# A block-causal attention with a squared-ReLU MLP on one core: the block products get banks of their own, v's scale two VectorE steps, the weight sums a later place, and the order list is planned anew

## The chip, the core and the metric

One core of a Trainium2 chip runs the whole program. The metric is the device time of one execution in microseconds (us). Engines are named as in the profile: PE is TensorE's matmul side and PEld its weight load, DVE is VectorE, ACT is ScalarE, POOL is GpSimd, SP issues the DMAs.

## The reference

Attention over 8 batches, 8 heads, 576 positions and 64 channels, with a mask by blocks of 64, and then an MLP without bias over the 4608 rows that come out:

```python
scores = scale * np.matmul(q, k.transpose(0, 1, 3, 2))
mask = block_i >= block_j
scores = np.where(mask, scores, -1000000000.0)
attn = np.exp(scores - np.max(scores, axis=-1, keepdims=True))
attn = attn / (np.sum(attn, axis=-1, keepdims=True) + 1e-09)
x = np.matmul(attn, v)            # to (4608, 512)
h = x @ w_in                      # (512, 2048)
r = np.maximum(h, 0.0)
out = (r * r) @ w_out             # (2048, 512)
```

q and k are drawn about five times larger than unit-scale noise of 0.1 would be; all is float32.

## The kernel before, in words

Every float32 operand of a large matmul is split in two float16 parts, high and low, and three products (high*high, high*low, low*high) stand for one float32 product. The work falls into 40 **passes** of attention (a pass is a pair of heads of one batch and some of the nine 64-row blocks) and 12 **chunks** of 384 rows of the MLP. Weights come in while the first passes run, are scaled, and are split too.

The order on each engine is a list. `plan_all` adds some 3,000 named steps, each with the engines that may take it, a duration in ns, the steps before it, a rank, and the buffer rings that it takes and frees; `Plan.run` walks through them with those durations and writes one list for each engine, and the compiled program keeps these lists. The constants at the top (`W0`, `YR`, `CHAIN`, `LOADS`, ...) are ranks and costs of this walk. Each engine works its list in order, so a step that waits holds up all that stand behind it.

Names of steps, with the tiles by which the profile shows them:

- In a pass i with groups g: `A` scores on PE into `side`; `B` row maxima on DVE (`nmx`); `C` exponentials on ACT (`p`), which also leave the sums; `S` on POOL (`sm`); `R` reciprocal on DVE (`rs`); from pass 12 on `H` and `L`, the high and low parts (`p_rows`), `T` their transposes by DMA (`p_turned`), and `G` the product with v on PE (`px`). In passes 0 to 11 `D` scales, `E` turns on PE, `F` copies back.
- v's scale, from pass 12 on: `fv` sums of |v| on ACT, `fa` a transpose on PE (`pm`), `fb` on DVE, `fc` a broadcast on PE, `fd` on DVE, then `vh` and `vl`, v's high and low parts (ACT and DVE). Before, `fb` is three DVE instructions (`mx` maximum, `mx` exponent mask, `dg`) and `fd` three more (`m`, `s`, `xsc`).
- Weights: `bits` on POOL, `prelu` on ACT, `join` on DVE rebuild the words; `w0a` to `w0e` and `w1a` to `w1e` make the scale of w_in and of w_out; `cast` and `low` split (DVE 0.5 and 0.7 us each).
- A chunk is **plain** (the first five of the order) or **split** (the other seven). Plain: `ph` (12 matmuls, `pair`), `pos`, `sqr`, `top`, `rem` (ACT and DVE, `r` and `hidden`), then `po` (48 matmuls for each third of the rows, 16 steps of 3), `ob` (scale, DVE) and `out` (store).
- Split chunks replace `ph` by seven block products for eight (a Strassen-Winograd scheme): in each of four groups `p1 p2 p6 p5 p7 p4 p3`, 12 matmuls each, into two banks, X and B. Between them copies take X (`c11`, `c12`, `c22`, `c21`) and additions take B (`a11`, `a22`, `a12`) to `r`: p6 adds to X once c11 has read it, p5 starts B anew once a11 has read it, and so on. The scheme wants sums of weight blocks, `t0_0` to `t3_12` and `t0_13` to `t3_17` (tile `_AluOpType.subtract`, on DVE or POOL).

The banks. PSUM has two tensors `side0` and `side1` of two banks each, `pair0` and `pair1` of one bank, and two banks of pool `ps_x`. From pass 14 on the scores use `side0` alone, and the block products turn through three banks, the halves of `side1` and `pair1`:

```python
homes = {"mm": pairs, "po": pairs[:1], "g": [sides[1][:, 0:512], sides[1][:, 512:1024], pairs[1]]}
```

Semaphores are set by the framework from what instructions read and write of a tensor, and the list's waits are what it finds.

Of the kernel before, what the change touches and what calls it, by code (L numbers as in the profile page):

```python
# [8 lines left out]
F32 = mybir.dt.float32  # L9
F16 = mybir.dt.float16  # L10
BF16 = mybir.dt.bfloat16
I32 = mybir.dt.int32
# [21 lines left out]
CALM = 537.27  # L34
# [19 lines left out]
W0 = (2.5, -14.69, -56.55, 10.59, 73.82, 23.78, 99.37)  # L54
W1 = (853.21, -0.0, -38.79, 11.96, -25.48)
NORMS = (7.15, -223.95)
YR = (62.35, -10.14, 23.9, -41.43)
UR = (281.66, -1.47, 123.95)
SLACK = 0
EARLY = 694.63  # L60
BEGIN = 334.95
FILLER = 10000
CHAIN = 138.99
FRONT = 239.18
MARGIN = 0
LATE = 167.03
LAND = 300
TURN = (699.23, 9.28)
LOADS = "z2 p0 r8 z1 r2 z0 r11 r1 r12 K1 r0 p1 r4 r5 r15 p2 p3 r14 K0 r3 z4 z5 Y0 z6 r13 Y1 r9 r10 r7 z3 r6"
# [64 lines left out]
class Plan:  # L134


    LAG = {"PE": 250, "DVE": 180, "ACT": 220, "POOL": 200, "SP": 100}
# [12 lines left out]
    def run(self):  # L150
# [63 lines left out]
def attention_moe_kernel(ctx: ExitStack, tc: tile.TileContext, qk1, v1, qk, ks, vm, vt, w_in, w_out, out):  # L214
# [12 lines left out]
    turns_of = dict.fromkeys(homes, 0)  # L227
# [255 lines left out]
    def front(t):  # L483
# [6 lines left out]
        def v_sum():  # L490
# [3 lines left out]
            box["steps"] = pow2_steps(box["st"], 1, u)  # L494

        def step(n):
            return lambda: box["steps"][n]()

        def scales():
            m = box["steps"][3]()  # L500
            box["s"] = scale_of(m, A_ATT, 1, u)
            xsc = t["xsc"] = small.tile([P, 1], F32, tag="xsc", name=f"xsc_{u}")
            nc.vector.tensor_scalar(xsc, m, 2.0 ** (-A_ATT - A_P), None, op0=ALU.mult)
# [5 lines left out]
        def v_low():  # L509
# [6 lines left out]
            v_sum=v_sum, turned=step(0), largest=step(1), spread=step(2), scales=scales, v_high=v_high, v_low=v_low  # L516
# [585 lines left out]
    def out_steps(ck, t):  # L1102
# [16 lines left out]
        def scaled(uv):  # L1119
            ob = box["ob"] = p2.tile([P, 512], F32, tag="ob", name=f"ob_{ck}_{t}", bufs=3)  # L1120
            nc.vector.tensor_scalar(
# [32 lines left out]
    def plan_all():  # L1154

        plan = Plan(
            {"s0": 1, "s1": 1, "mm": 2, "x": 2, "p32": 2, "ks": 2, "v16": 2, "g": 3, "po": 1, "qk": 2, "r": 8, "hb": 2, "ob": 3, "dg": 1}
# [56 lines left out]
        def part_steps(wi, f, early, rank):  # L1214
# [23 lines left out]
            add(f"prelu{k}", "ACT", 610, [raw] + back, early, start, takes)  # L1238
# [7 lines left out]
            add(f"low{k}", "DVE", 750, [f"cast{k}"], rank, lambda: box["s"][3](), frees=ends)  # L1246

        def row_steps(t, k, group, rank, after, frees, parts):
# [12 lines left out]
            score = 0.9 * w + 120 if t["quad"] else 880 if short else 1.68 * w + 80 * n - 20  # L1261
# [9 lines left out]
            add(f"R{k}", "DVE", 190, [f"S{k}"], rank, get("inverse"))  # L1271
# [157 lines left out]
        def moe(n):  # L1429
# [7 lines left out]
            for g in range(0 if plain(ck) else NQ):  # L1437
# [27 lines left out]
                for name, after in (("11", f"p1{k}"), ("12", f"p6{k}"), ("22", f"p7{k}")):  # L1465
                    add(f"c{name}{k}", {"ACT": 440, "DVE": 480}, 0, [after], r, step("c" + name), ("r",))
                add(f"a11{k}", "DVE", 560, [f"p2{k}", f"c11{k}"], r, step("a11"))
                add(f"a22{k}", "DVE", 560, [f"p5{k}", f"c22{k}"], r, step("a22"))
                add(f"a12{k}", "DVE", 560, [f"p3{k}", f"c12{k}"], r, step("a12"), frees=[(f"p2{k}", "g")])
                add(f"c21{k}", {"ACT": 440, "DVE": 480}, 0, [f"p4{k}"], r, step("pos"), ("r",), frees=[(f"p1{k}", "g")])  # L1470
                for name in ("11", "21", "22", "12"):
                    first = f"c21{k}" if name == "21" else f"a{name}{k}"
                    add(f"sq{name}{k}", {"ACT": 540 if name == "21" else 1050, "DVE": 520}, 0, [first], CALM, step("s" + name))
# [5 lines left out]
            for f in range(NF if plain(ck) else 0):  # L1479
# [17 lines left out]
                add(f"pos{k}", "ACT", 500, [f"ph{k}"], r, step(1), ("r",), frees=[(f"ph{k}", "mm")])  # L1497
                add(f"sqr{k}", "ACT", 550, [f"pos{k}"], r, step(2))
# [6 lines left out]
            for m in range(3):  # L1505
# [6 lines left out]
                for f in range(NF):  # L1512
# [11 lines left out]
                    f"ob{ck}_{m}", "DVE", 730, [f"po{ck}_{m}_15", f"uv{ck}"], CHAIN, lambda box=box: box["s"][1](uv["a"]),  # L1524
# [12 lines left out]
        for n in range(NQ):  # L1537
# [72 lines left out]
        for t in passes[WHOLE:]:  # L1610
# [27 lines left out]
            add(f"fb{i}", "DVE", 620, [f"fa{i}"], r, go("largest"), ("dg",))  # L1638
            add(f"fc{i}", "PE", 100, [f"fb{i}"], r, go("spread"), frees=[(f"fb{i}", "dg")])
            add(f"fd{i}", "DVE", 470, [f"fc{i}"], r, go("scales"), frees=[(f"fa{i}", "x")])  # L1640
            ready_rows = [f"load{i}"]
            slots = [(f"load{i}", x) for x in ("qk", "ks")]
            add(f"vh{i}", "ACT", 720, [f"fd{i}"], r + (2 if early else 20), go("v_high"))
# [82 lines left out]
```

## Time and profile before

| | us |
|---|---|
| runs, median of 3 | 1044.79 (1043.6 to 1045.23) |
| profiled execution, its own time | 1046.3 |
| its span, first to last instruction | 1044.5 |
| PE busy | 976.9 (94%) |
| DVE busy | 818.7 (78%) |
| ACT busy | 572.4 (55%) |
| POOL busy | 168.7 (16%) |

The profiled execution is 1.5 us above the median of the runs, and 1.8 us of its time lie outside the span. Busy time is the union of an engine's instructions. A matmul row lasts until its modelled end, and the next starts before that, so back-to-back matmuls overlap in the rows.

### The profile page before, as it was taken

The numbers are of one execution on the slowest core, as the hardware profiler recorded it, in microseconds if no ns is written. First come the engines' busy times: TensorE is split into PE (matmuls) and PEld (weight loads), VectorE is DVE, ScalarE is ACT, GpSimd is POOL, SyncE is SP. The second block draws the span as 40 slices with busy tenths as digits, with TensorE's granted clock in tenths as the row PEclk, the third lists the DMA queues.
The fourth block names the chain that finished last, engine by engine and source line by source line (L and its number), as shares of the span: only waits on it lengthen the run. The fifth ranks groups of instructions, "written<-read, shape, count | busy, mean of one in ns | idle before, by whom it ended". The sixth has DMA issues, their size and how long they took to land.

```text
span 1044.5 us, 20623 instructions
## 1 busy us (share of the span) xinstructions
PE 976.9 (94%) x7889; PEld 591.9 (57%) x7889; DVE 818.7 (78%) x1974; ACT 572.4 (55%) x1451; POOL 168.7 (16%) x252
## 2 busy tenths in 40 slices
PE   6679998899999999998999999999999999989998
PEld 5445533444554554554476485586575485486673
DVE  7999899898788777879789687799788787665350
ACT  5888715763874685475455465456566446233130
POOL 3443334220110010003012011011001001011010
PEclk9689999999999999999999999999999999999999
DMA  9852206855665667641624603841963533500001
GB/s 354 311 172 95 96 11 153 184 113 118 143 147 132 148 114 161 131 110 60 144 50 106 135 12 81 177 104 24 211 128 56 112 84 50 98 11 12 21 1 31
DMA packets 216611, 114.86 MB, mean 110 GB/s; under 512 B 190400, under 2 KB 198592, under 8 KB 216512
## 3 DMA queue, kind: packets, MB, share of 16 engines
q1 hardware_dynamic: 216512, 113.54, 44.8%
q8 instruction: 62, 1.02, 0.4%
q14 instruction: 37, 0.30, 0.1%
HBM read 58.20 MB, written 9.44 MB: 65 GB/s over the span
## 4 chain that ended last, share of the span: by engine, by line
PE 61%; DVE 20%; issue 9%; ACT 5%; DMA 2%; POOL 1%; SPq 0%; POOLq 0%; DVEq 0%; ACTq 0%
PE pair L106 37%; PE side L106 18%; PE px L106 5%; DVE w L106 4%; DVE p_rows L106 4%; DVE r L106 3%; DVE nmx L106 3%; ACT r L106 2%; DVE xt_all L106 1%; DMA p_turned<-p_rows 1%; ACT p L106 1%; DVE hidden L106 1%; PE po L106 1%; DVE _AluOpType.subtract L106 1%; DMA w<-in_w_in 1%
## 5 line engine op out<-in xcount | busy, mean ns | idle before, releaser
L106 PE MATMUL pair<-w,hidden 128*128 128x512 f16 x1680 | 384.5, 380 | 2.8 <-DVE ob L106 1.5
L106 PEld LDWEIGHTS <-hidden 128*128 128x128 f16 x1728 | 162.3, 98 | 194.4 <-issue 15.6
L106 PEld LDWEIGHTS <-w 128*128 128x128 f16 x2304 | 203.5, 98 | 97.9 <-issue 38.6
L106 PE MATMUL pair<-xt_all,w 128*128 128x384 f16 (+1 forms) x1392 | 209.5, 304 | 2.6 <-DVE xt_all L106 1.7
L106 ACT ACTIVATE p<-side,nmx 128x256 f32<-128x256 f32 (+8 forms) x264 | 139.6, 539 | 123.2 <-DVE nmx L106 74.4
L106 DVE TENSOR_REDUCE nmx<-side 128x1 f32<-128x64 f32 (+8 forms) x288 | 123.2, 480 | 13.5 <-PE side L106 13.5
L106 DVE SCALAR_TENSOR_TENSOR p_rows<-p,rs,p_rows 128x64 f16<-128x64 f32 (+6 forms) x264 | 133.0, 548 | 0.6
L106 POOL TENSOR_SCALAR sm<-sm 128x2 f32<-128x2 f32 (+2 forms) x104 | 31.2, 300 | 512.7 <-ACT p L106 494.0
L106 ACT CAST hidden<-r 128x384 f16<-128x384 f32 x181 | 91.5, 510 | 35.9 <-DVE r L106 32.2
L106 PE MATMUL side<-qk 64*64 64x512 f32 (+1 forms) x480 | 98.6, 506 | 10.6 <-ACT p L106 9.6
L106 PE MATMUL side<-xt_all,w 128*128 128x192 f16 x912 | 86.2, 246 | 13.3 <-DVE r L106 8.7
L106 PE MATMUL side<-ks,qk 64*64 64x192 f32 (+4 forms) x576 | 93.1, 429 | 0.0
L106 DVE TENSOR_TENSOR hidden<-r,hidden 128x384 f16<-128x384 f32 x144 | 80.0, 562 | 14.1 <-ACT hidden L106 13.0
L106 PEld LDWEIGHTS <-turned_w 128*128 128x128 f16 x1008 | 84.1, 98 | 10.6 <-issue 7.8
L106 POOL TENSOR_TENSOR hidden<-r,hidden 128x384 f16<-128x384 f32 x48 | 48.5, 1015 | 232.8 <-ACT hidden L106 206.8
L106 DVE TENSOR_SCALAR p_rows<-p,rs 128x256 f16<-128x256 f32 (+10 forms) x198 | 76.2, 423 | 2.5
L106 ACT ACTIVATE r<-pair 128x384 f32<-128x384 f32 x106 | 51.6, 489 | 45.2 <-PE pair L106 44.9
L106 PE MATMUL px<-p_turned,v 128*64 128x384 f16 (+5 forms) x1168 | 71.6, 270 | 4.1 <-ACT x L106 1.7
L106 ACT ACTIVATE r<-side 128x384 f32<-128x384 f32 x55 | 26.6, 490 | 85.8 <-PE side L106 80.3
L106 PE MATMUL side<-xt_all,turned_w 128*128 128x192 f16 x684 | 65.1, 246 | 4.6 <-ACT r L106 2.4
L106 DVE TENSOR_SCALAR ob<-pair,uv 128x512 f32<-128x512 f32 x35 | 28.3, 808 | 51.9 <-PE pair L106 51.5
L106 PEld LDWEIGHTS <-v 128*64 128x64 f16 x1128 | 51.4, 110 | 28.3 <-issue 18.8
(149 smaller groups left out, 1126.6 us busy)
## 6 DMA issues: line engine op xcount, KB each, us to landing
qk<-in_qk SPq DMA_DIRECT2D x32, 576.0 KB, 4.5
ks<-in_ks SPq DMA_DIRECT2D x32, 320.0 KB, 4.7
vraw<-in_vm SPq DMA_DIRECT2D x30, 256.0 KB, 5.0
w<-in_w_out SPq DMA_DIRECT2D x10, 512.0 KB, 5.2
out<-ob SPq DMA_DIRECT2D x20, 256.0 KB, 2.0
w<-in_w_in SPq DMA_DIRECT2D x8, 512.0 KB, 8.4
hidden<-in_w_in SPq DMA_DIRECT2D x6, 512.0 KB, 9.9
out<-ob SPq DMA_DIRECT2D x24, 128.0 KB, 2.5
```

The lines of the kernel that those rows point to most:

```text
L106: i = make(*a, **k)
```

## The change

Four things. (1) `side1` and `pair1` move to a pool that is closed at the first block product, and three tensors `group0` to `group2` of one bank each take their place. (2) v's scale: DVE keeps the maximum (`fb`) and one mask step (`fd`), and three small instructions go to POOL as a new step `fe`. (3) The first weight sum waits for the end of pass 16 (`X16_1`). (4) The plan has other durations, new constants and ranks, a penalty of 98.64 ns on DVE where a step may go to several engines (`EASE`), a charge on DVE for paired POOL work (`DRAG`), another order of loads, 500 ns more between a step and a PE step of rank 300 or more (`MARGIN`, `LATE`), and `ob` may go to ACT as two passes.

```diff
-MARGIN = 0
-LATE = 167.03
+DRAG = 0.3
+LATER = 16
+EASE = 98.64
+MARGIN = 500
+LATE = 300
-LOADS = "z2 p0 r8 z1 r2 z0 r11 r1 r12 K1 r0 p1 r4 r5 r15 p2 p3 r14 K0 r3 z4 z5 Y0 z6 r13 Y1 r9 r10 r7 z3 r6"
+LOADS = "p0 p1 p2 r1 p3 r0 Y0 r3 r4 r5 r2 z0 r6 K0 r10 r7 r11 r13 r9 r12 K1 r8 z1 z2 r14 r15 Y1 z3 z6 z4 z5"
...
-                if best is None or at + queues[q] < best[0]:
-                    best = at + queues[q], at, q
+                cost = at + queues[q] + (EASE if q == "DVE" else 0)
+                if best is None or cost < best[0]:
+                    best = cost, at, q
...
+            if q == "POOL" and name.startswith(self.PAIRED) and free["DVE"] > at:
+                free["DVE"] += DRAG * queues[q]
...
-    sides = [ps_b.tile([P, 1024], F32, name=f"side{n}") for n in range(2)]
-    pairs = [ps_b.tile([P, 512], F32, name=f"pair{n}") for n in range(2)]
-    homes = {"mm": pairs, "po": pairs[:1], "g": [sides[1][:, 0:512], sides[1][:, 512:1024], pairs[1]]}
+    early = ExitStack()
+    ps_e = early.enter_context(tc.tile_pool(name="ps_e", bufs=1, space=PSUM))
+    sides.append(ps_e.tile([P, 1024], F32, name="side1"))
+    pairs.append(ps_e.tile([P, 512], F32, name="pair1"))
+    homes = {"mm": pairs, "po": pairs[:1]}
...
+        if ring not in homes:
+            early.close()
+            ps_g = ctx.enter_context(tc.tile_pool(name="ps_g", bufs=1, space=PSUM))
+            homes[ring] = [ps_g.tile([P, 512], F32, name=f"group{n}") for n in range(3)]
...
+        def largest():
+            box["top"] = small.tile([1, 1], BF16, tag="top", name=f"top_{u}", bufs=1)
+            nc.vector.tensor_reduce(box["top"], box["pm"][:1, :P], axis=AX.X, op=ALU.max)
...
+        def read():
+            m = box["m"] = small.tile([P, 1], F32, tag="m", name=f"m_{u}")
+            nc.vector.tensor_scalar(
+                m.bitcast(I32), box["pm"][:, P : P + 1].bitcast(I32), EXPMASK, None, op0=ALU.bitwise_and
+            )
...
+            nc.gpsimd.tensor_scalar(m, m, 2.0**-100, None, op0=ALU.max)
...
+            if q == "ACT":
+                nc.scalar.activation(ob, box["po"], AF.Copy, scale=uv[:, 0, t : t + 1])
+                nc.scalar.activation(ob, ob, AF.Copy, scale=uv[:, 1, t : t + 1])
+                return
...
-                    after += [...] + (["low1_15"] + [f"max1_{f}" for f in range(NF)] if n == 0 else [])
+                    after += [...] + (["low1_15"] + [f"max1_{f}" for f in range(NF)] + [f"X{LATER}_1"] if n == 0 else [])
```

Where the lists move, at three places. First DVE's list around the end of pass 15 and the start of pass 16, before; `p_rows` rows are H and L, `nmx` is B, and the `t_AluOpType.subtract` and `turned_w` rows are weight sums of group 3:

```order
L106 TENSOR_TENSOR t_AluOpType.subtract_2354<-t_AluOpType.subtract_2354,w_99 128x512 x2
L106 RECIPROCAL rs_3_3_4_2384<-sm_3_3_4_2357 128x2
...
L106 SCALAR_TENSOR_TENSOR p_rows<-p_1_3_3_4_2356,rs_3_3_4_2384,p_rows 128x256
L106 TENSOR_TENSOR turned_w<-t_AluOpType.subtract_2354,turned_w 128x2x256
L106 TENSOR_TENSOR t_AluOpType.subtract_2354<-t_AluOpType.subtract_2354,w_99 128x512 x2
L106 TENSOR_REDUCE nmx_0_0_4_2416<-side_73 128x1 x4
L106 TENSOR_SCALAR nmx_0_0_4_2416<-nmx_0_0_4_2416 128x4
L106 TENSOR_TENSOR turned_w<-t_AluOpType.subtract_2354,turned_w 128x2x256
L106 TENSOR_TENSOR t_AluOpType.subtract_2354<-w_99,t_AluOpType.subtract_2354 128x512
L106 TENSOR_TENSOR t_AluOpType.subtract_2354<-t_AluOpType.subtract_2354,w_99 128x512
```

The same place of DVE's list now:

```order
L109 RECIPROCAL rs_3_3_4_2265<-sm_3_3_4_2237 128x2
L109 TENSOR_SCALAR p_rows<-p_1_3_3_4_2236,rs_3_3_4_2265 128x320
L109 TENSOR_SCALAR p_rows<-p_1_3_3_4_2236,rs_3_3_4_2265 128x256
L109 SCALAR_TENSOR_TENSOR p_rows<-p_1_3_3_4_2236,rs_3_3_4_2265,p_rows 128x320
L109 TENSOR_TENSOR hidden<-r_10_2256,hidden 128x384
L109 SCALAR_TENSOR_TENSOR p_rows<-p_1_3_3_4_2236,rs_3_3_4_2265,p_rows 128x256
L109 SCALAR_TENSOR_TENSOR v_2_0_0_2201<-vraw_86,s_0_0_2261,v_2_0_0_2201 128x640
L109 TENSOR_REDUCE nmx_0_0_4_2301<-side_73 128x1 x4
```

The weight sums are gone from here; they stand behind pass 16. Up to the last low part of pass 16 (L16_2_1) the list of before has 20 of them on DVE, that of now none; POOL's list has 20 of the first 52 of these steps before and 27 now.

Second, DVE's list at v's scale in pass 14. Before, six instructions:

```order
L106 TENSOR_REDUCE mx_2_3_1910<-pm_2_3_1891 1x1
L106 TENSOR_SCALAR mx_2_3_1910<-mx_2_3_1910 1x1
L106 TENSOR_SCALAR dg_2_3_1913<-ident,mx_2_3_1910 1x1
...
L106 TENSOR_SCALAR m_2_3_1941<-pm_2_3_1891 128x1
L106 TENSOR_SCALAR s_2_3_1943<-m_2_3_1941 128x1
L106 TENSOR_SCALAR xsc_2_3_1945<-m_2_3_1941 128x1
```

Now two, with other work between them, and m, s and xsc are three rows of POOL's list:

```order
L109 TENSOR_REDUCE top_2_3_1861<-pm_2_3_1702 1x1
L109 TENSOR_REDUCE nmx_2_3_8_1866<-side_73 128x1 x2
L109 TENSOR_SCALAR nmx_2_3_8_1866<-nmx_2_3_8_1866 128x2
L109 TENSOR_TENSOR sq_1_0_1843<-sq_1_0_1843 128x384
L109 TENSOR_SCALAR m_2_3_1882<-pm_2_3_1702 128x1
```

Third, PE's list with its waits in the split chunk 8, where p2 of group 3 (`p28_3`) starts. Before, it stands right behind p3 of group 2, which goes to `pair`:

```order
L106 LDWEIGHTS w_99
L106 MATMUL pair_76<-xt_all,w_99 128x192
L106 LDWEIGHTS w_99
L106 MATMUL side_74<-xt_all,w_99 128x192 [waits Activation_49]
L106 LDWEIGHTS w_99
L106 MATMUL side_74<-xt_all,w_99 128x192
```

Now p2 of group 3 stands behind p1 of group 3, p5 of group 2 and a small `nq` product:

```order
L109 MATMUL group_5469<-xt_all,w_102 128x192
L109 LDWEIGHTS ones_bf
L109 MATMUL nq_1_9386<-sq_1_0_9165,ones_bf 128x384 [waits DVE_49]
L109 LDWEIGHTS ones_bf
L109 MATMUL nq_1_9386<-sq_1_2_9316,ones_bf 128x384 [waits DVE_49]
L109 LDWEIGHTS w_102
L109 MATMUL group_5468<-xt_all,w_102 128x192 [waits Activation_49]
```

Followed to the instruction whose count the semaphore reaches, the wait of before is for the copy c12 of group 3, which reads the other half of `side1`; the wait of now is for c21 of group 2, the last reader of p2's own bank. The products' own work is the same in both lists.

## Rows read from the trace of the kernel before

**Rows 1.** Busy time by stretch (us: PE, PEld, DVE, ACT, POOL; PE's clock, DMA).

```profile
0.00:265.00 265.00, 227.64 (x1567) 124.29 (x1571) 241.69 (x538) 170.69 (x442) 83.73 (x120) 0.94 0.54 161
265.00:488.00 223.00, 220.92 (x1653) 116.60 (x1645) 177.41 (x468) 142.92 (x367) 27.14 (x45) 1.00 0.58 129
488.00:1044.50 556.50, 528.31 (x4676) 351.01 (x4674) 399.63 (x970) 258.79 (x643) 57.85 (x87) 1.00 0.36 78
```

**Rows 2.** The chain that ended last (start, us, what): steps of PE.

```profile
114.48 1.95 PE pair L106 x12
...
262.56 2.19 PE px L106 x42
...
1030.14 10.37 PE pair L106 x48
```

**Rows 3.** PE's waits from 488 to 1044.5 us: in total, times, longest.

```profile
PE side L106 <- DVE r L106: 10.9, 23, 1.1
PE side L106 <- ACT r L106: 7.0, 13, 1.1
...
PE pair L106 <- DVE ob L106: 1.5, 3, 0.6
```

**Rows 4.** Timeline of chunk 8: block products, and copies on ACT (start, us, what).

```profile
779.81 1.15 PE L106 MATMUL side<-xt_all,w 128*128 128x192 f16 x12
780.80 1.15 PE L106 MATMUL pair<-xt_all,w 128*128 128x192 f16 x12
...
784.98 0.49 ACT L106 ACTIVATE r<-side 128x384 f32<-128x384 f32 x1 [2.23 <-PE side L106]
...
786.48 0.48 ACT L106 ACTIVATE r<-side 128x384 f32<-128x384 f32 x1
787.01 1.15 PE L106 MATMUL side<-xt_all,w 128*128 128x192 f16 x12 [1.08 <-ACT r L106]
```

**Rows 5.** DVE's groups by form, 170 to 254 us (count, busy us, mean ns, idle).

```profile
L106 DVE TENSOR_TENSOR _AluOpType.subtract<-_AluOpType.subtract,w 128x512 f32<-128x512 f32 x10 | 6.9, 691 | 0.3
L106 DVE SCALAR_TENSOR_TENSOR p_rows<-p,rs,p_rows 128x384 f16<-128x384 f32 x4 | 4.3, 1064 | 0.0
L106 DVE TENSOR_SCALAR p_rows<-p,rs 128x320 f16<-128x320 f32 x4 | 3.2, 795 | 0.1
L106 DVE TENSOR_SCALAR ob<-pair,uv 128x512 f32<-128x512 f32 x3 | 2.4, 801 | 0.7 <-PE pair L106 0.7
```

**Rows 6.** DVE's groups by form, whole span: small steps of v's scale.

```profile
L106 DVE TENSOR_SCALAR dg<-ident,mx 1x1 bf16<-1x1 f32 x28 | 5.7, 204 | 1.0
L106 DVE TENSOR_SCALAR s<-m 128x1 int32<-128x1 int32 x28 | 4.3, 154 | 1.0
L106 DVE TENSOR_SCALAR xsc<-m 128x1 f32<-128x1 f32 x28 | 4.0, 144 | 0.0
L106 DVE TENSOR_SCALAR mx<-mx 1x1 int32<-1x1 int32 x28 | 4.0, 142 | 1.0
```

**Rows 7.** DVE's timeline: the first scores' maxima, the first reciprocal, the last split of w_out.

```profile
5.70 0.69 DVE L106 TENSOR_REDUCE nmx<-side 128x1 f32<-128x192 f32 x3 [4.09 <-PE side L106]
12.87 0.16 DVE L106 RECIPROCAL rs<-sm 128x3 f32<-128x3 f32 x1
139.76 0.75 DVE L106 SCALAR_TENSOR_TENSOR w<-turned_w,wsc,w 128x512 f16<-128x512 f32 x1
```

**Rows 8.** ACT by form, whole span: one pass over 512 columns.

```profile
L106 ACT ACTIVATE wt<-hidden 128x512 f32<-128x512 f32 x6 | 3.9, 671 | 0.0
```

**Rows 9.** POOL by form, whole span: a small step, and a weight sum.

```profile
L106 POOL TENSOR_SCALAR sm<-sm 128x2 f32<-128x2 f32 x48 | 15.4, 320 | 237.8 <-ACT p L106 231.9 <-DVE hb L106 5.6
L106 POOL TENSOR_TENSOR _AluOpType.subtract<-_AluOpType.subtract,w 128x512 f32<-128x512 f32 x10 | 14.0, 1401 | 2.2 <-DVE _AluOpType.subtract L106 0.8 <-DVE rs L106 0.8
```

**Rows 10.** DVE by form, whole span: H over 320 columns. And the 50 us from 150.

```profile
L106 DVE TENSOR_SCALAR p_rows<-p,rs 128x320 f16<-128x320 f32 x23 | 10.5, 457 | 0.7
...
150.00:200.00 50.00, 43.14 (x269) 20.74 (x269) 45.45 (x95) 27.71 (x63) 21.39 (x20) 0.93 0.59 138
```

More of the change, by code (lines that the diff above doesn't have):

```diff
@@ L33 @@
 ALONE = 14
-CALM = 537.27
+CALM = 17.25
 A_ATT = 14
@@ L493, in v_sum, with turned, spread @@
             nc.scalar.activation(t["v16"][:, 0, :, 0:c, :], v32, AF.Abs, accum_out=box["st"])
-            box["steps"] = pow2_steps(box["st"], 1, u)
-        def step(n):
-            return lambda: box["steps"][n]()
-        def scales():
-            m = box["steps"][3]()
-            box["s"] = scale_of(m, A_ATT, 1, u)
+        def turned():
+            pm = box["pm"] = ps_x.tile([P, 512], F32, tag="x", name=f"pm_{u}")
+            nc.tensor.transpose(pm[:1, :P], box["st"], ident)
+        def largest():
+            box["top"] = small.tile([1, 1], BF16, tag="top", name=f"top_{u}", bufs=1)
+            nc.vector.tensor_reduce(box["top"], box["pm"][:1, :P], axis=AX.X, op=ALU.max)
+        def spread():
+            nc.tensor.matmul(box["pm"][:, P : P + 1], ones_bf[:1], box["top"], start=True, stop=True)
+        def read():
[3 more added lines that the diff above has]
+            )
+        def scales():
+            m = box["m"]
+            nc.gpsimd.tensor_scalar(m, m, 2.0**-100, None, op0=ALU.max)
+            s = box["s"] = small.tile([P, 1], F32, tag="s", name=f"s_{u}")
+            nc.gpsimd.tensor_scalar(
+                s.bitcast(I32), m.bitcast(I32), -1, (254 + A_ATT) << 23, op0=ALU.mult, op1=ALU.add
+            )
             xsc = t["xsc"] = small.tile([P, 1], F32, tag="xsc", name=f"xsc_{u}")
-            nc.vector.tensor_scalar(xsc, m, 2.0 ** (-A_ATT - A_P), None, op0=ALU.mult)
+            nc.gpsimd.tensor_scalar(xsc, m, 2.0 ** (-A_ATT - A_P), None, op0=ALU.mult)
         def v_high():
@@ L515, in front @@
         return dict(
-            v_sum=v_sum, turned=step(0), largest=step(1), spread=step(2), scales=scales, v_high=v_high, v_low=v_low
+            v_sum=v_sum, turned=turned, largest=largest, spread=spread, read=read, scales=scales, v_high=v_high, v_low=v_low
         )
@@ L1237, in part_steps @@
             add(f"bits{k}", "POOL", 800, [raw], early + 10, lambda: low_bits(raws[wi][f]))
-            add(f"prelu{k}", "ACT", 610, [raw] + back, early, start, takes)
+            add(f"prelu{k}", "ACT", 580, [raw] + back, early, start, takes)
             add(
@@ L1245, in part_steps @@
             add(f"cast{k}", {"ACT": 630, "DVE": 520, "POOL": 1600}, 0, [f"join{k}", f"w{wi}e"] + last, rank, lambda q: box["s"][2](q))
-            add(f"low{k}", "DVE", 750, [f"cast{k}"], rank, lambda: box["s"][3](), frees=ends)
+            add(f"low{k}", "DVE", 700, [f"cast{k}"], rank, lambda: box["s"][3](), frees=ends)
         def row_steps(t, k, group, rank, after, frees, parts):
@@ L1465, in moe @@
                 for name, after in (("11", f"p1{k}"), ("12", f"p6{k}"), ("22", f"p7{k}")):
[L1466 to L1470, printed above, removed]
+                    add(f"c{name}{k}", {"ACT": 400, "DVE": 480}, 0, [after], r, step("c" + name), ("r",))
+                add(f"a11{k}", "DVE", 480, [f"p2{k}", f"c11{k}"], r, step("a11"))
+                add(f"a22{k}", "DVE", 480, [f"p5{k}", f"c22{k}"], r, step("a22"))
+                add(f"a12{k}", "DVE", 480, [f"p3{k}", f"c12{k}"], r, step("a12"), frees=[(f"p2{k}", "g")])
+                add(f"c21{k}", {"ACT": 400, "DVE": 480}, 0, [f"p4{k}"], r, step("pos"), ("r",), frees=[(f"p1{k}", "g")])
                 for name in ("11", "21", "22", "12"):
                     first = f"c21{k}" if name == "21" else f"a{name}{k}"
-                    add(f"sq{name}{k}", {"ACT": 540 if name == "21" else 1050, "DVE": 520}, 0, [first], CALM, step("s" + name))
+                    add(f"sq{name}{k}", {"ACT": 440 if name == "21" else 880, "DVE": 520}, 0, [first], CALM, step("s" + name))
                     add(f"top{name}{k}", {"ACT": 440}, 0, [f"sq{name}{k}"] + over[name], r, lambda name=name, step=step: step("h" + name)("ACT"))
@@ L1637, in plan_all @@
             add(f"fa{i}", "PE", 120, [f"fv{i}"], r, go("turned"), ("x",))
[L1638 to L1640 removed]
+            add(f"fb{i}", "DVE", 210, [f"fa{i}"], r, go("largest"), ("top",))
+            add(f"fc{i}", "PE", 100, [f"fb{i}"], r, go("spread"), frees=[(f"fb{i}", "top")])
+            add(f"fd{i}", "DVE", 130, [f"fc{i}"], r, go("read"), frees=[(f"fa{i}", "x")])
+            add(f"fe{i}", "POOL", 800, [f"fd{i}"], r, go("scales"))
             ready_rows = [f"load{i}"]
             slots = [(f"load{i}", x) for x in ("qk", "ks")]
[L1643 removed]
+            add(f"vh{i}", "ACT", 720, [f"fe{i}"], r + (2 if early else 20), go("v_high"))
             add(f"vl{i}", "DVE", 800, [f"vh{i}"], r + (2 if early else 20), go("v_low"))
```

41 lines of the change are left out of this document (22 added, 19 removed).

## The prediction, made before the changed kernel was run

> **What bounds the kernel now.** I read busy time by stretch first [rows 1]; the reader is to see three regimes. Up to 265 us TensorE is busy for 227.6 us and VectorE for 241.7 (91%): this front is VectorE's. From 265 to 488 us TensorE is busy for 220.9 of 223.0 and nothing can be gained but what is in the list itself. From 488 us on, where the split chunks run, TensorE is idle for 556.5 - 528.3 = 28.2 us although VectorE has 157 us to spare. Then the chain that ended last [rows 2], which gives what a step costs when nothing waits: 48 matmuls of `po` in 10.37 us, so 0.648 for a step of three, and 1.95 for a `ph`. Then TensorE's waits in the last stretch [rows 3]: 36 waits of block products for copies of `r` make 17.9 of the 28.2 us. Last the timeline of one of them [rows 4], to see for which copy it waits.
>
> All changes keep TensorE's work, so only its waiting can change. Ahead of any step, its waiting is the step's start less the work that its list has before it. Summing the list, each kind at its unhindered start-to-start time, gives 199.6 us ahead of the product of pass 16; that starts at 262.56 [rows 2], so 63 us have been lost by then. The whole list is 929 us. The other losses are 7 us up to 488 and 41 after it (the part by which these exceed the idle time is the overlap of products described next).
>
> **Banks of their own.** Products stand 0.99 us apart but each lasts 1.15 [rows 4], so a wait costs its idle time and also 0.16 us of lost overlap: 17.9 + 36 * 0.16 = 23.7 us. Of what are these waits made? At 787.01 us p2 of group 3 starts, 0.05 us after an ACT copy that began at 786.48; but the last reader of the bank that it writes is the copy that ended at 785.47 [rows 4]. The list with waits in the section on the change says why: the two halves of `side1` are one tensor to the framework, and the wait is for a reader of the other half. I followed all waits of block products to the instruction that they name: about 35 name a copy that their own bank does not ask for, and had each product started when its own copy was done (or the product ahead of it), 18.5 us would have been kept. The lists of now have no such wait. The other 5 us are true waits (p4 behind c22, p2 behind c21), and here the new order counts. Between p7 and p4, 8 of the 28 groups of before have a single product (0.99 us) and between p4 and the p2 that takes its bank 11 have; a copy of 0.49 us on ACT [rows 4] plus hand-over and queueing does not always fit. Now the smallest distances are 1.45 and 1.98 us. I take 20 of 23.7 us as gained; bounds are 12 (the copies come late for other reasons and true waits replace false ones) and 23.7.
>
> Closing the pool adds one wait: the first product after the last readers of `side1` and `pair1`. It already waits for the last plain chunk, whose copies they are; 0, or one copy (0.5 us) without that cover.
>
> **The front.** Two places decide, and I work both by what is put ahead of them.
> At pass 16: up to its last low part VectorE's list loses 28.9 us of steps and gains 11.0. Gone are 20 weight sums, about 0.69 us each [rows 5] (13.7); 8 high parts at some 0.7 (5.7); five copies to `p_turned` (2.7), 3 `ob` at 0.80 [rows 5] (2.4), two `D` (1.8), six smaller (2.5). New are as many copies, high parts, casts and others that came the other way. v's scale drops 0.142 + 0.204 + 0.154 + 0.144 = 0.64 us a pass [rows 6], 3.2 for passes 12 to 16. Together 21.1 us less. But TensorE's list also has 21 `po` steps less ahead, 21 * 0.648 = 13.6 us [rows 2]. So TensorE has lost 63 - (21.1 - 13.6) = 55.5 us there.
> At the end of w_out's splits: these now stand behind the L steps of most of pass 13. The list ahead of the last one is longer by 12 L (8.8), 6 B (8.0), 6 H (4.4), chunk 1's operand (8.1), two `vl` (2.7) and others, about 35 us net. It started at 139.76 and took 0.75 [rows 7], so it would end at 175.6. The `po` step that needs it (chunk 0, first third, last step) has 96.4 us of TensorE's work ahead before and 22.5 more now, 5 `ph` [rows 2] and 6 `po` among it: 175.6 - 118.9 = 57 us lost. This is the tighter place.
> Two things are still to be set against each other. The weight sums on POOL from 150 us on (POOL is busy 21.4 of 50 [rows 10]) stretch VectorE's steps: H over 320 columns takes 795 ns there [rows 5] against 457 over the whole span [rows 10]; without them some 2 us come back before the tighter place. And the early list has the first reciprocal right behind the second scores' maxima; today 7.2 us lie between the first maxima and that reciprocal [rows 7], so VectorE will wait at first, 0 to 6 us, of which I take 2 (w_in's loads would hold it up anyway). The lost time stays at 57, a gain of 63 - 57 = 6 us, between 0 and 15.
>
> **Behind the front.** TensorE's other waits are 28.2 - 17.9 = 10.3 us after 488 and 2.1 between 265 and 488 [rows 1, 3]. The plan's 500 ns more ahead of TensorE's late steps puts other work between a result and its use; I take 3 us, bounds 0 and 6.
> The small cost terms: nine of 36 `ob` go to ACT as two passes, 2 * 0.67 [rows 8] against 0.80 [rows 5], so 0.5 us later each. It is hidden where the next third's products run in another bank; `po` has one bank in the split chunks, where three waits for `ob` make 1.5 us today [rows 3]. I take 1 us, at worst 9 * 0.5 = 4.5. `fe` is three POOL steps of about 0.32 [rows 9], 1 us instead of 0.3 on VectorE, so v's parts come 0.7 us later. The row steps that stand between `fd` and `vl` in VectorE's list cover it; without the cover it would be 28 * 0.7 = 20 us on VectorE, which from 265 us on has over 20% to spare.
>
> **The sum.** 20 + 6 + 3 - 1 = 28 us. The profiled execution took 1046.3, so 1018.3; the median of the runs is 1.5 lower, so 1016.8, or **1017 us**.
>
> **Shared port, a rule against the change.** VectorE's 457 against 795 ns show that POOL's weight sums slow VectorE [rows 5, 10]. The Trainium skill, "SBUF — State Buffer", section "Who interferes with whom", says that VectorE and GpSimd share one pair of ports and that the second to come is blocked for the whole instruction; the trace agrees in direction. By that rule moving the sums moves the blocking with them.
>
> **The rivals.**
> - Collision behind pass 16. Of the first 52 weight sums 27 are now on POOL (20 before), at 1.4 us [rows 9] between about 245 and 330 us, each able to hold up VectorE by 0.34 us (795 - 457) or more (an L over 384 columns took 1064 ns [rows 5]): 9 to 15 us. For it: VectorE is only just ahead of TensorE up to pass 20. Against: from 265 us on it has 45 of 223 us free [rows 1]. The front's 6 us and 6 more would go: 1029 us.
> - Only the false waits go. The front gains nothing (VectorE falls behind its list early, as the reciprocals suggest), and the new distances give nothing: 18.5 - 1 = 17.5, so 1027 us.
> - The separate banks give little: the copies that products need end at the same time, since ACT and VectorE work their lists in order and are late themselves. Then about a third of 23.7 remains a gain: 8 + 6 = 14, so 1031 us.
> - Slower: w_out's splits come too late. The second layer of chunk 0 cannot start before them, and it stands behind 35 us more of VectorE's work than now. If VectorE lags its list by more than 28 us there (57 + 28 = 85, which eats 6 and 22), the kernel is slower, by 1 us for each us of lag; 35 us of lag would give 1052. For it: a chain of eight passes with a wait at each reciprocal. Against: VectorE idles only 23 us in the whole front of before [rows 1].
> - Better: the front gains at both places as much as POOL gives back, 12 to 15 us, and all block waits go: 1045 - 15 - 23 - 5 = 1002 to 1008 us.
>
> **How the numbers follow.** The forecast (1011 to 1022) 0.48; the better case 0.17; only false waits or collision (1022 to 1030) 0.22; little from the banks (1030 to 1038) 0.07; no change or slower 0.06. Leaving out the ends gives 1004 to 1031 us for 8 in 10. A change within 0.2% (2 us) could not be told from none; faster by more 0.94, within 0.02, slower 0.04.
>
> **What would show it.** TensorE's waits for `r` in the last half fall from 36 to under 12, and their sum below 5 us; the rows say `group` in place of `side`. VectorE's busy share stays at 90% up to some 215 us and falls before 265; the `po` steps of chunk 0 run at about 155 to 185 us, in step with w_out's splits. The product of pass 16 starts near 242 us and the first block product near 480 (488 now). If the first stretch ends late or VectorE idles more than 25 us in it, the front's step is wrong; if waits for `r` stay above 12 us, that of the banks.

## The result, and the profile after

The changed kernel takes 1010.65 us (median of 4 runs, 1010.31 to 1012.81), the one before 1044.68 in the same comparison: a ratio of 0.968, 95% interval 0.9663 to 0.9697, so faster by 34 us. The profiled execution took 1010.31 us with a span of 1008.5; against the profiled execution of before the span is 36.0 us shorter, and the accounts below are made against these 36.0. Times of the runs below are medians of their fast runs; the kernel without the 500 ns had two more runs, of 1641 and 2682 us, that are left out.

Busy time by stretch of the changed kernel, columns as in [rows 1] (us, then the stretch; PE, PEld, DVE, ACT, POOL; PE's clock, DMA):

```profile
0.00:265.00 265.00, 238.22 (x1717) 128.83 (x1718) 233.36 (x538) 184.91 (x480) 71.62 (x132) 0.97 0.61 173
265.00:488.00 223.00, 214.58 (x1559) 114.21 (x1559) 182.29 (x406) 145.28 (x360) 52.04 (x80) 0.98 0.52 116
488.00:1008.50 520.50, 514.42 (x4625) 345.40 (x4621) 376.85 (x885) 268.94 (x667) 56.71 (x116) 1.00 0.38 83
```

TensorE is now busy for 10.6 us more in the first stretch, idles 8.4 us in the second (2.1 before), and 6.1 in the third (28.2 before). Its waits in the third stretch, as in [rows 3]:

```profile
PE pair L109 <- DVE ob L109: 0.9, 1, 0.9
PE px L109 <- DMA p_turned<-p_rows: 0.4, 1, 0.4
PE group L109 <- DVE xt_all L109: 0.3, 1, 0.3
PE group L109 <- DVE r L109: 0.3, 1, 0.3
PE px L109 <- DVE ivs L109: 0.2, 1, 0.2
```

Of 36 waits for `r` and 17.9 us, one of 0.3 us is left. The timeline of chunk 8, to be read against [rows 4] (start, us, what):

```profile
764.60 1.15 PE L109 MATMUL group<-xt_all,w 128*128 128x192 f16 x12
765.09 0.48 ACT L109 ACTIVATE r<-group 128x384 f32<-128x384 f32 x1
765.70 1.15 PE L109 MATMUL group<-xt_all,w 128*128 128x192 f16 x12
766.03 0.47 ACT L109 ACTIVATE r<-group 128x384 f32<-128x384 f32 x1
767.01 1.15 PE L109 MATMUL group<-xt_all,w 128*128 128x192 f16 x12
```

The last row is p2 of group 3, the step that started 0.05 us behind the end of a copy from the other half in [rows 4]. Now its bank's last reader (c21 of group 2, the first ACT row) has ended at 765.57, long before, and no wait stands at its row; the small `nq` product lies between it and p5.

The chain that ended last has the product of pass 16 at 232.62 us (262.56 in [rows 2]):

```profile
232.62 1.84 PE px L109 x30
...
472.69 2.01 DVE _AluOpType.subtract L109 x2
...
476.70 1.68 DVE xt_all L109
478.42 3.83 PE group L109 x23
```

That is 29.9 us earlier (in [rows 2] twelve matmuls of the pass's smaller product, under half a us, are in the same row), 13.6 of which are the 21 `po` steps that now stand behind it; 16.3 us are time no longer lost. The first block product starts at 474.44, and did at 488.3: 13.9 us, so 2.4 of the 16.3 are given back between the two. From there to the end it is 534.1 us against 556.2: 22.1 us less, although the chain shows a new wait at its beginning. In TensorE's timeline:

```profile
474.44 0.25 PE L109 MATMUL group<-xt_all,w 128*128 128x192 f16 x1
478.42 0.80 PE L109 MATMUL group<-xt_all,w 128*128 128x192 f16 x4 [3.73 <-DVE xt_all L109]
```

The second matmul of the first block product needs a low part of x that stands in VectorE's list behind the last weight sums. This wait costs more than its 3.73 us. TensorE idles from 474.7 to 478.4 us, and for 477 to 484 us the granted clock is 0.51, the lower of its two levels (1.2 GHz); it is 1.00 in the 7 us before and behind:

```profile
477.00:484.00 7.00, 5.58 (x28) 4.07 (x28) 6.17 (x10) 2.44 (x5) 1.86 (x2) 0.51 0.10 37
```

So 36.0 = 16.3 - 2.4 + 22.1, and the 22.1 hold this wait and the slower matmuls behind it.

Two of VectorE's rows that answer to [rows 7], the first reciprocal and the last split of w_out:

```profile
8.04 0.18 DVE L109 RECIPROCAL rs<-sm 128x3 f32<-128x3 f32 x1 [0.58 <-POOL sm L109]
...
162.24 0.75 DVE L109 SCALAR_TENSOR_TENSOR w<-turned_w,wsc,w 128x512 f16<-128x512 f32 x1
```

### The profile page after: what moved, and what is told of

Same layout as the page of the kernel before. It is cut to its first block, busy times and chain, and to the rows that moved or that the text cites. A ratio compares the mean times of both kernels' runs of the same rounds, so it can differ in the third digit from the quotient of the medians.

```text
span 1008.5 us, 20543 instructions
## 1 busy us (share of the span) xinstructions
PE 967.2 (96%) x7889; PEld 588.4 (58%) x7889; DVE 792.5 (79%) x1828; ACT 599.1 (59%) x1507; POOL 180.4 (18%) x327
## 4 chain that ended last, share of the span: by engine, by line
PE 71%; DVE 14%; ACT 6%; DMA 5%; issue 2%; POOL 1%; SPq 0%; DVEq 0%; POOLq 0%; ACTq 0%
PE pair L109 37%; PE group L109 19%; PE side L109 7%; PE px L109 6%; DVE w L109 3%; DVE p_rows L109 3%; DMA p_turned<-p_rows 2%; ACT p L109 2%; DVE nmx L109 2%; DMA w<-in_w_in 2%; ACT r L109 2%; DVE xt_all L109 1%; PE po L109 1%; DVE _AluOpType.subtract L109 1%; ACT hidden L109 1%
## 5 line engine op out<-in xcount | busy, mean ns | idle before, releaser
L109 PEld LDWEIGHTS <-w 128*128 128x128 f16 x2304 | 204.5, 98 | 83.7 <-issue 16.8
L109 ACT ACTIVATE p<-side,nmx 128x448 f32<-128x448 f32 (+8 forms) x264 | 139.4, 537 | 106.5 <-DVE nmx L109 87.4
L109 PE MATMUL pair<-xt_all,w 128*128 128x384 f16 x960 | 165.9, 328 | 3.9 <-DVE w L109 2.7
L109 DVE TENSOR_REDUCE nmx<-side 128x1 f32<-128x192 f32 (+8 forms) x288 | 123.2, 479 | 11.1 <-PE side L109 10.8
L109 PE MATMUL group<-xt_all,w 128*128 128x192 f16 x1344 | 126.2, 248 | 4.3 <-DVE xt_all L109 4.0
L109 DVE TENSOR_TENSOR hidden<-r,hidden 128x384 f16<-128x384 f32 x166 | 94.8, 576 | 25.9 <-ACT hidden L109 24.1
L109 PE MATMUL group<-xt_all,turned_w 128*128 128x192 f16 x1008 | 95.4, 246 | 0.0
L109 PE MATMUL side<-ks,qk 64*64 64x192 f32 (+4 forms) x576 | 91.7, 424 | 0.0
L109 PEld LDWEIGHTS <-turned_w 128*128 128x128 f16 x1008 | 83.7, 98 | 6.7 <-issue 2.0
L109 ACT ACTIVATE r<-group 128x384 f32<-128x384 f32 x90 | 43.9, 488 | 63.1 <-PE group L109 62.4
L109 DVE TENSOR_SCALAR p_rows<-p,rs 128x320 f16<-128x320 f32 (+10 forms) x192 | 77.0, 441 | 3.3 <-DMA p_turned<-p_rows 0.3
L109 ACT ACTIVATE r<-r 128x384 f32<-128x384 f32 x125 | 65.4, 523 | 8.3 <-DVE r L109 4.9
L109 ACT ACTIVATE p_rows<-p,rs 128x448 f16<-128x448 f32 (+8 forms) x96 | 45.1, 503 | 23.4 <-DVE rs L109 22.8
L109 ACT ACTIVATE x<-px,xsc 128x384 f32<-128x384 f32 (+1 forms) x52 | 26.3, 506 | 54.3 <-PE px L109 49.1
```

Source lines behind the costliest of these rows:

```text
L109: i = make(*a, **k)
```

## The experiments

Two theories stand behind the forecast: the block products waited for readers of banks that were not theirs, and the front is VectorE's, with its list of steps as the price. The rivals are that copies come late anyway, and that something other than the list's length made the front.

**The banks.** One kernel has the old lists and new banks, one the new lists and old banks. The edit of the first (the second is its reverse in the changed kernel):

```diff
-    homes = {"mm": pairs, "po": pairs[:1], "g": [sides[1][:, 0:512], sides[1][:, 512:1024], pairs[1]]}
+    homes = {"mm": pairs, "po": pairs[:1]}
...
+            homes[ring] = [ps_g.tile([P, 512], F32, name=f"group{n}") for n in range(3)]
```

> The kernel before with one thing of the change, the three banks of the block products as tensors of their own; all lists are those of before. My theory: the 36 waits of block products for copies are nearly all for a reader of the other half of one tensor, so they go, with 0.16 us of overlap each: 18 to 23 us less, 1022 to 1027 us, TensorE's waits for r below 5 us in sum. Rival, the banks give little since the copies themselves come late: about 8 us less, 1037 us, and the waits for r stay above 10 us.

Measured: 1018.08 us, ratio 0.9742 (0.9727 to 0.9756). The stretch from 488 us, and the waits in it:

```profile
488.00:1016.40 528.40, 519.52 (x4654) 348.44 (x4651) 397.98 (x966) 256.13 (x641) 56.78 (x87) 1.00 0.38 82
```

```profile
PE px L106 <- ACT x L106: 1.7, 1, 1.7
PE pair L106 <- DVE ob L106: 1.5, 4, 0.6
PE side L106 <- ACT p L106: 0.7, 1, 0.7
PE pm L106 <- DVE dg L106: 0.6, 1, 0.6
PE px L106 <- DMA p_turned<-p_rows: 0.2, 1, 0.2
```

The view lists no wait for `r` any more, in the old order. 26.6 us, more than either theory gave.

> The changed kernel with the block products' banks as before (two halves of one tensor, and a third tensor shared with the plain chunks); all lists are those of the changed kernel. My theory: the order of the new list does not help a wait that names the wrong copy, so 12 to 20 us come back, 1023 to 1031 us. Rival, the larger distances of the new list (1.45 and 1.98 us at least instead of 0.99) cover most of such waits: 2 to 6 us come back, 1013 to 1017 us.

Measured: 1026.84 us, 0.983 (0.9813 to 0.9848), so 16 us come back. The waits from 488 us:

```profile
PE side L109 <- DVE r L109: 7.3, 15, 0.8
PE side L109 <- ACT r L109: 4.1, 14, 0.6
```

With shared banks the new order still has 29 waits. It shortens them (11.4 us in place of 17.9) and does not remove them; the rival of a list that is enough by itself is out.

**The weight sums on GpSimd, in the old front.** The edit leaves them out on GpSimd alone (three of the last sums, behind 456 us, went with them; one fill stays where a sum opens a tile or makes a low part). The kernel computes with wrong weight sums; VectorE's and TensorE's lists are those of before to the step:

```diff
-            return lambda q: tt(q, x, y, op)
+            return lambda q: tt(q, x, y, op) if q == "DVE" else None
...
```

> The kernel before without the weight sums that GpSimd does ahead of the block products (20 of 52; a fill with a constant stands where a sum opened a tile or made a low part, so the block products get wrong operands); all lists stay. Theory, contention: VectorE's steps beside these sums are stretched by about 11 us in all, so the product of pass 16 starts 8 to 13 us earlier (at 250 to 255 us) and the time falls to 1032 to 1037 us. Rival, the order of the list made the front's gain and not the contention: pass 16 starts at most 3 us earlier, 1041 to 1045 us.

Measured: 1026.83 us, 0.9827 (0.9812 to 0.9842): 17.8 us less. The product of pass 16 starts 18.1 us earlier than in [rows 2]:

```profile
244.50 2.26 PE L106 MATMUL px<-p_turned,v 128*64 128x192 f16 x42
```

and the rows of VectorE's groups from 170 to 254 us answer to those of [rows 5], 1064 and 795 ns in the mean:

```profile
L106 DVE SCALAR_TENSOR_TENSOR p_rows<-p,rs,p_rows 128x384 f16<-128x384 f32 x4 | 2.4, 610 | 0.0
...
L106 DVE TENSOR_SCALAR p_rows<-p,rs 128x320 f16<-128x320 f32 x4 | 1.5, 386 | 0.1
```

The means of [rows 5] mix steps beside a sum with others. Of the four high parts of 320 columns there two start while a sum runs and take 1.09 and 1.32 us, and two take 0.39; of the four low parts of 384 columns two take 1.52 us and two 0.61. In the kernel before, the high parts (of 320 and of 256 columns) of pass 13, beside sums, and of pass 15:

```profile
178.64 2.59 POOL L106 TENSOR_TENSOR _AluOpType.subtract<-_AluOpType.subtract,w 128x512 f32<-128x512 f32 x2
179.09 2.29 DVE L106 TENSOR_SCALAR p_rows<-p,rs 128x320 f16<-128x320 f32 x2
...
225.21 0.65 DVE L106 TENSOR_SCALAR p_rows<-p,rs 128x320 f16<-128x320 f32 x2
```

Summed over the 364 steps that VectorE has up to the last low part of pass 16, the same steps in the same order take 257.9 us with the sums and 242.4 without: 15.5 us for 20 sums on another engine, 0.78 each. More than the 8 to 13 that I expected, and the rival (3 us at most) is out.

But leaving steps out also makes GpSimd less busy, and VectorE might have waited for its small steps. So the same kernel again, with three fills in place of each sum:

```diff
+        def filled(o):
+            for _ in range(3):
+                nc.gpsimd.memset(o, 1.0)
...
-            return lambda q: tt(q, x, y, op)
+            return lambda q: tt(q, x, y, op) if q == "DVE" else filled(box["t"])
...
```

> The kernel before with each of the 20 early weight sums of GpSimd replaced by three fills with a constant, 1.5 us in all where a sum took about 1.4 (the block products get wrong operands); all lists stay, and GpSimd is as busy as before. Theory: what slows VectorE is that a sum reads two operands beside VectorE's steps, so fills cost little, 1027 to 1031 us, pass 16 at 245 to 249 us, as in the run without the sums. Rival: it is GpSimd's occupation, since VectorE waits for GpSimd's own late steps, or since any GpSimd step blocks VectorE; then 1037 to 1045 us, pass 16 at 255 to 263 us.

Measured: 1028.95 us, 0.9857 (0.9839 to 0.9875), with the product of pass 16 at

```profile
248.11 2.26 PE L106 MATMUL px<-p_turned,v 128*64 128x192 f16 x42
```

GpSimd's fills from 125 to 205 us, and then VectorE's two groups from 170 to 254 us:

```profile
L106 POOL MEMSET _AluOpType.subtract<- 128x512 f32 x36 | 20.5, 568 | 2.5 <-DVE _AluOpType.subtract L106 0.7
```

```profile
L106 DVE SCALAR_TENSOR_TENSOR p_rows<-p,rs,p_rows 128x384 f16<-128x384 f32 x4 | 2.4, 610 | 0.0
...
L106 DVE TENSOR_SCALAR p_rows<-p,rs 128x320 f16<-128x320 f32 x5 | 2.4, 471 | 0.2
```

GpSimd is busy for 91.7 us up to 265 us (83.7 before), and 14.5 of the 18.1 us at pass 16 stay gained. It is not GpSimd's occupation; it is what a sum does while VectorE works. A step of VectorE with two operands (the low part) runs beside fills as if GpSimd did nothing; one with a single operand (the high part) is still slowed by fills, 471 against 386 ns in the mean (two of the five stand beside fills and take 0.55 and 0.65 us), but less than by sums.

**The sums behind pass 16.** In the changed kernel GpSimd has 27 of the first 52 sums behind pass 16. The edit that left out the early sums, made in the changed kernel (three of the last sums went with them here too):

```diff
-            return lambda q: tt(q, x, y, op)
+            return lambda q: tt(q, x, y, op) if q == "DVE" else None
...
```

> The changed kernel without the 27 weight sums that GpSimd does behind pass 16 (constants in their place, so wrong operands again); all lists stay. Theory: the sums behind pass 16 give back about 3 us, so 1006 to 1009 us, with pass 16 at the same 232 us. Rival, the collision costs 9 to 15 us there and is only hidden by other gains: 996 to 1002 us. Second rival, GpSimd's sums are free there since TensorE is the bound: 1010 us.

Measured: 1002.16 us, 0.9589 (0.9574 to 0.9604), 8.5 us less, between the two theories. From 233 to 350 us the changed kernel and this one:

```profile
233.00:350.00 117.00, 112.74 (x832) 59.02 (x828) 103.49 (x212) 74.97 (x189) 43.99 (x53) 1.00 0.48 110
```

```profile
233.00:350.00 117.00, 117.00 (x874) 61.27 (x867) 90.28 (x223) 76.67 (x193) 15.56 (x41) 1.00 0.52 115
```

TensorE's 4.3 us of idle time go, and 13 us of VectorE's busy time. The first block product starts 3.3 us earlier, at 471.17. What comes behind it belongs, by VectorE's rows, to the three last sums and not to the 27 (no run leaves out the three alone): in the changed kernel they run on GpSimd from 462.8 to 469.5 us, and without them VectorE's steps between 455 us and the low part of x are 2.5 us shorter. So the wait there shrinks from 3.7 to 1.4 us, and TensorE's clock stays at its upper level (1.00 from 470 to 490 us):

```profile
472.80 2.06 PE L109 MATMUL group<-xt_all,w 128*128 128x192 f16 x23 [1.39 <-DVE xt_all L109]
```

From the start of this row to that of the next `px` product TensorE takes 6.5 us here, and 9.2 in the changed kernel for the same matmuls: 2.7 us are the clock. So 3.3 us of the gain are those of the 27 sums, and 2.3 + 2.7, the wait and the clock, those of the three last ones.

**Sums back in the front.** The changed kernel without the wait for pass 16:

```diff
-  after += [...] + [f"max1_{f}" for f in range(NF)] + [f"X{LATER}_1"] if n == 0 else [])
+  after += [...] + [f"max1_{f}" for f in range(NF)] if n == 0 else [])
```

> The changed kernel without the wait of the weight sums for pass 16; the list then puts about 36 of them between the end of w_out's splits and pass 16, a dozen on VectorE, the others on GpSimd. Theory: each of GpSimd's costs VectorE about 0.75 us and each of VectorE's 0.7, so pass 16 comes 15 to 24 us later, of which the 8.5 us lost behind pass 16 are not lost again: 1017 to 1027 us. Rival: the loss only changes place, 1009 to 1013 us.

Measured: 1018.57 us, 0.9755 (0.9739 to 0.977), 8 us more. The product of pass 16 starts at

```profile
246.04 1.91 PE L109 MATMUL px<-p_turned,v 128*64 128x384 f16 x30
```

13.5 us later than in the changed kernel (232.55 in its timeline), of which 1.3 are two more `po` steps ahead of it: 12.2 us are lost there. The loss does not only change place, and the theory's lower end is met.

**v's scale.** First the changed kernel with the old steps (the maximum, a mask and a diagonal; then m, s and xsc, all on VectorE; `fe` empty):

```diff
-            nc.vector.tensor_reduce(box["top"], box["pm"][:1, :P], axis=AX.X, op=ALU.max)
+            box["steps"][1]()
...
```

> The changed kernel with v's scale computed as before (three small VectorE steps for the maximum, three for the scale, none on GpSimd); all lists are those of the changed kernel. Theory: 0.64 us a pass more on VectorE, which is the bound only up to pass 16, five passes: 2 to 4 us come back, 1012.5 to 1015 us, with pass 16 as much later. Rival, other VectorE waits or GpSimd's three small steps cost as much as they saved: within 1 us of 1010.7.

Measured: 1015.03 us, 0.9723 (0.9708 to 0.9738): 4.4 us more, the theory's upper end, but not where it said. The product of pass 16 starts only 0.9 us later:

```profile
233.49 1.91 PE L109 MATMUL px<-p_turned,v 128*64 128x384 f16 x30
```

and the first block product 3.1 us later, at 477.5. Most of it is lost between these two: from 233 to 350 us TensorE is busy for 110.95 us, 112.74 in the changed kernel, so VectorE's list still holds it up there.

Then the kernel before with the new steps (and their own durations) and the new banks, all other numbers for the list as they were:

```diff
-            add(f"fd{i}", "DVE", 470, [f"fc{i}"], r, go("scales"), frees=[(f"fa{i}", "x")])
+            add(f"fd{i}", "DVE", 130, [f"fc{i}"], r, go("read"), frees=[(f"fa{i}", "x")])
+            add(f"fe{i}", "POOL", 800, [f"fd{i}"], r, go("scales"))
...
```

> The kernel before with the banks of their own and v's scale in two VectorE steps, without the new numbers of the list and without the wait for pass 16. Theory: the 4.3 us of v's scale add to the 26.6 us of the banks, since VectorE is the bound of the front: 1012 to 1016 us. Rival: the old front is held up by GpSimd's weight sums and three more steps on GpSimd come late, so v's scale brings nothing: 1017 to 1020 us.

Measured: 1019.63 us, 0.9771 (0.9753 to 0.9789), not better than the banks alone: the rival's time, but not by its way. Pass 16 comes 4.5 us earlier than with the banks alone (256.6 and 261.1 us). The list that comes out around the shorter steps gives it back; from 480 us on TensorE waits for

```profile
PE pair L106 <- DVE ob L106: 4.1, 4, 1.4
PE group L106 <- ACT r L106: 3.2, 2, 2.9
```

**The 500 ns.** The changed kernel with one number as before:

```diff
-MARGIN = 500
+MARGIN = 0
```

> The changed kernel without the 500 ns more that the list asks ahead of TensorE's late steps. Theory: with banks of their own the block products wait for nothing, so these 500 ns matter little: 0 to 1.5 us more, 1010 to 1012 us. Rival, my term of 3 us: waits for copies and for ob come back in the last half, 1013 to 1015 us.

Measured: 1017.6 us, 0.9746 (0.9728 to 0.9764), some 7 us more, which neither theory has. The block products still wait for little, as the banks would have it (0.8 us for `r`). The time goes earlier: the product of pass 16 starts 4.1 us later, and from 240 to 490 us TensorE waits for

```profile
PE side L109 <- ACT p L109: 3.3, 3, 1.9
PE iv L109 <- DVE hb L109: 2.3, 1, 2.3
PE nq L109 <- DVE sq L109: 1.4, 2, 0.7
```

Some 400 of VectorE's 1443 steps stand at another place of its list by this one number, so the 7 us are those of another list, not of the distance alone; which part is which stays open.

**Better than both.** Three versions of the changed kernel. First, the last weight sums of block rows 1 to 3 ranked behind the operands of the first split chunk:

```diff
-                    f"t{n}_{x}", ways, 0, after, TURN[x > 12], ...
+                    f"t{n}_{x}", ways, 0, after, TURN[x > 12] if x < 13 or not n else 9000 + n, ...
```

> The changed kernel with the last weight sums of block rows 1 to 3 ranked behind the operands of the first split chunk, so that the low part for which the first block product waits stands seven VectorE steps earlier. Theory: the wait of 3.7 us behind the first block product goes and nothing takes its place, 1006 to 1008 us. Rival, the next product then waits for these sums, or VectorE is just as late elsewhere: 1009.5 to 1012 us.

Measured: 1009.02 us, 0.9662 (0.9648 to 0.9676), inconclusive beside the changed kernel's 0.968. The wait of 3.7 us is gone and the clock stays at 1.00, but the first block product starts 1.7 us later, at 476.14, and from 474 to 500 us there is another wait:

```profile
PE pair L109 <- DVE ob L109: 2.8, 1, 2.8
```

Second, with GpSimd's cost for the first 52 sums set out of reach as well:

```diff
-                ways = ({"POOL": 1800, "DVE": 660}, ...)[kind]
+                ways = ({"POOL": 1800 if x > 12 else 90000, "DVE": 660}, ...)[kind]
```

> As the last one, and the first 52 weight sums behind pass 16 may go to VectorE only, none to GpSimd (27 were on GpSimd): 18 us more work for VectorE, which idles about 40 us between 265 and 488 us. Theory, the sharing between GpSimd and VectorE makes the loss behind pass 16: without it the loss goes, 5 to 8 us less than the changed kernel beside the 3 us of the late sums, 1000 to 1004 us. Rival, VectorE's 18 us more cost as much as the sharing: 1006 to 1010 us.

Third, with the first step's rank, GpSimd's cost as it was, and

```diff
-LATER = 16
+LATER = 20
```

> As the run with the late sums, and the weight sums wait for pass 20 in place of 16 (the list then puts nearly all of the first 52 on VectorE, 1 on GpSimd). Theory: VectorE is ahead of TensorE by then, so the sums cost nothing: 1000 to 1004 us, and the first plain chunks behind pass 16 start as early as without any sums. Rival: packed between pass 20 and the first block product they make VectorE late there, 1006 to 1012 us.

Measured: 1005.85 us, 0.9637 (0.9624 to 0.965), for the second, and **1004.71 us, 0.9622 (0.9609 to 0.9635)** for the third, the fastest here that computes the whole of the reference, though the two are not clear of each other. From 233 to 350 us the third:

```profile
233.00:350.00 117.00, 117.00 (x883) 60.98 (x879) 87.09 (x216) 75.52 (x192) 7.80 (x28) 1.00 0.59 133
```

TensorE has no idle time there, as without the sums. Both times lie between those of the two theories: from 440 to 520 us TensorE now waits 3.7 and 3.2 us for ACT's `p`, and the new lists lose something elsewhere that I did not follow.

## Why the prediction was right, and what was mis-sized

The direction, the two causes and the outer range (1004 to 1031) held; the forecast of 28 us was 6 to 8 short, and 1010.65 lies just outside the forecast's own band (1011 to 1022), between it and the better case. In the prediction's terms 20 + 6 + 3 - 1 became, by the profiled executions, 25.9 for the banks, 16.3 - 2.4 for the front, 2.6 for other waits, and 6.4 us lost at a wait that nobody had counted: 36.0. That two terms were too small and a loss was left out made the sum closer than its parts; this much is luck.

- **Banks: 20 us predicted, bounds 12 and 23.7; about 25.9 measured.** With new banks alone, 556.2 us from the first block product on become 530.3. The false waits were right. Wrong was the step "The other 5 us are true waits (p4 behind c22, p2 behind c21), and here the new order counts": with banks of their own the old order has none of these waits. I took 20 of 23.7 on their account, and even 23.7 was short: TensorE's busy time from 488 us falls by 8.8 us, where I counted 36 times 0.16, 5.8, of overlap (2.2 us of work are done ahead of 488 there, though). The new list then gives 3.8 back in this stretch, 22.1 in place of 25.9: the wait at the first block product costs 3.73 us and the clock behind it 2.7, and 2.6 us are gained elsewhere.
- **The front: 6 us predicted, bounds 0 and 15; 16.3 at pass 16, 13.9 at the first block product.** The mis-sized term is "without them some 2 us come back before the tighter place". Leaving GpSimd's sums out of the old front gave 18.1 us at pass 16 and 15.5 us of VectorE's durations, more than the whole change gained there: these sums are enough for all of the front's gain. What it brings alone that VectorE's own 20 sums left the front was not run. By count the last split of w_out would have ended at 175.6; it did at 163.0, since VectorE's steps ahead of it took 11 us less than the same steps in the run of before, and the lag of 2 us at the start did not come (the first reciprocal is at 8.04, 12.87 in [rows 7]). I had both rows for this, 1064 and 795 against 457 ns, and read them short in two ways. I priced them for the few steps ahead of the tighter place rather than for all that VectorE does while the sums run, from 126 to 221 us. And these are means over steps with and without a sum beside them, so 795 - 457 = 0.34 us is not what a sum costs a step; the steps beside one were 0.7 to 0.9 us longer.
- **The collision behind pass 16**, a rival at 9 to 15 us, is real but smaller: without these 27 sums the first block product starts 3.3 us earlier, which is about the 2.4 us that the front's gain shrinks up to there. The other 5 us of that run hang on the three last sums, which also lengthen VectorE's steps, and on TensorE's clock.
- **Other waits: 3 us predicted; 2.6 found in the last stretch.** Without the waits for `r`, those that the views list from 488 us on are 4.7 us with the new banks alone and 1.8 in the changed kernel. But the new list has made the wait at the first block product, 6.4 us with the clock, so nothing of this is left in the sum. With the number back at 0 the list costs some 7 us more, but ahead of the block products, not at the late steps for which I priced it.
- **`ob` on ACT, 1 us lost:** not run alone. Nine went to ACT; TensorE's waits for `ob` in the last stretch are 0.9 us, 1.5 in [rows 3], so no loss is seen.
- **v's scale, 3.2 us for five passes:** 4.4, but mostly behind pass 16. No run shows a loss by `fe`.
- **What would show it:** the waits for `r` and the name `group` came as said; chunk 0's `po` run from 143 to 180 us (155 to 185 said), the product of pass 16 and the first block product come 9 and 6 us earlier than said. VectorE's busy share did not stay at 90% up to 215 us: it is 42.14 us of the 50 from 150.

The parts do not add. Banks alone give 26.6 us, all but the banks 17.8, the whole 34. Of the 10 us between, 6.5 are false waits that the new list shortens (17.9 to 11.4 us of idle time) and that are gone anyway with the new banks; the rest I did not follow.

## What to carry to other kernels

Look at what a wait names, not at how long it is: two halves of one tensor are one tensor to the framework, and giving each bank its own name was worth more than any new order. An engine that stands beside a bound engine is not free because it is idle: price its steps by what they do to the other's durations, over every step that overlaps, by leaving them out once, and not by a group's mean, which mixes steps that overlap with steps that do not. A wait of TensorE can cost more than its length, if its clock falls in it. A gain at one place is measured with the other parts in and out, since a planned list changes everywhere when one number does.

## What the runs showed of the hardware

Twenty sums of 1.2 to 2.6 us on GpSimd lengthened VectorE's steps by 15.5 us; I had expected 2 ahead of the tighter place. A two-operand step (a low part of 384 columns) took 1.52 us when it started while a sum ran, and 0.61 beside fills of some 0.57 us and alone. A one-operand step (a high part of 320 columns) took 1.09 and 1.32 us beside sums, 0.55 and 0.65 beside fills and 0.39 alone. The Trainium skill, "SBUF — State Buffer", section "Who interferes with whom", says that a VectorE instruction with two operands in SBUF contends with a GpSimd instruction that reads SBUF, not with one that only writes it, and that `tensor_scalar` may contend in its two-port modes. These rows agree on both. As I put the section's rule in the prediction, without these conditions, fills should have blocked the two-operand steps as well; they did not.

An idle time of 3.73 us at the first block product, with TensorE's granted clock at 0.51 from 477 to 484 us behind it, made the same matmuls take 9.2 us; with an idle time of 1.39 us there, in the run without the sums on GpSimd, the clock was 1.00 and they took 6.5.
